# A chunked linear attention and two feed-forward layers: decay products with a floor inside the scan, and the first layer's opening blocks in turns

## The chip, the cores and the metric

One of the eight cores of a Trainium2 chip runs the whole program. The metric is the device time of one execution in microseconds (us). Engines are named as in the profile: PE is the matrix engine, PEld its weight load, DVE the vector engine, ACT the scalar engine, POOL GpSimd, and SP the engine whose queue issues all the DMAs of this kernel.

## The reference

Three stages follow one another on 3072 tokens (4 batches of 768) of width 384 (8 heads of 48).

```python
for t in range(S):                       # 768 steps, for each of 4 batches and 8 heads
    state = alpha[:, :, t, :, None] * state + einsum('bhd,bhe->bhde', k[:, :, t], v[:, :, t])
    y[:, :, t] = einsum('bhd,bhde->bhe', q[:, :, t], state)
x = y in token order, 384 wide
h = x @ w_in                             # 384 -> 2048
g = (a0 + a1 h + a2 h^2 + a3 h^3) / (1 + |b0| |h| + |b1| h^2 + 1e-6)
x = g @ w_out                            # 2048 -> 384
h = x @ w_in2;  out = (h * cos(h)) @ w_out2
```

alpha lies between 0.8 and 1. The weights arrive as 64-bit floats.

## The kernel before

**Attention.** The sequence is cut into 6 chunks of 128 steps; a chunk of one batch is one unit, so there are 24. Inside a unit, heads lie as 4 pairs (HP) on 128 partitions. decay makes the running product p of the decays along the chunk, four rows of 128 in one tensor_tensor_scan (L246): state = a * state + fresh, where fresh is 0 but for each row's first column, which holds the row's first decay (and a[..., 0] is 0, so the scan starts anew there). guess1 (L261) writes max(p, 2^-60) to the bank r and sums it; guess2 (L268, L269) turns r into exp(-ln r) on ACT and sums that; inverse0 (L276) and inverse1 (L284) refine the inverse by one step, and inverse0 sums r * p. q is multiplied by p (scale_q, L293) and k by the inverse (scale_k, L288), both on POOL, after which a unit is a masked product of scores plus a product with the state. The sums go to three rows of chk; all_ok0 and all_ok1 test them in units 16 and 18 of the layers and set a flag. Were it set, a general path (general) would run after the fast one.

attention(n, tick) writes one turn of this pipeline: for unit n the scores, for n+1 scale_q, the inverse and scale_k, for n+2 the guesses, for n+3 the decay, for n-1 and n-2 the output and the update of the state. The order on each engine is the order of the program text, written by hand; every engine works through its own queue in that order.

**Layers.** Two layers of 96 units each: 6 blocks of 512 tokens, and for each block 16 groups of 128 features. A unit is gemm1 (9 matmuls at L478: weights and x each split into a high and a low part, three products over three slices of 128) and, five units later in the first layer and four in the second, gemm2 (9 matmuls at L491 into three accumulators acc0 to acc2). Between them, rational or cosine work on the unit's 128 x 512 values on DVE, ACT and POOL, spread over the following units; L539 is the last reader of a unit's bank b0, b1 or b2, which gemm1 takes again three units on. At a block's end acc_out copies the accumulators and stores them. x of the next block is loaded by x_load and split by x_hi (ACT) and x_lo (DVE, L603). The layers' unit 0 is written right behind attention unit 20 (LEAD), so attention units 20 to 24 and layer units 0 to 4 are interleaved.

**Weights.** Each of 64 weight tiles (128 x 384, 64 bit) is fetched by w_fetch into one of four slots of a spare x tile or one of two raw tiles, turned to 32 bit in three steps (step 0: L66 and L67 on ACT; step 1: L71 and step 2: L72 on DVE), and split into high (L182, ACT) and low (L191, POOL). tick(k, ahead) takes up to k steps where it stands, as long as more than ahead tiles are under way. During the attention, step 0 writes to the one bank words_t; from unit 0 of the layers on, the steps work in SBUF alone until the second layer. w_order is the order of the tiles: for the first layer, feature i of w_in and feature i - 4 of w_out side by side. The first 16 tiles of the second layer are parked in DRAM (wd), with kq_t and v_t as staging, and loaded back by w_load from unit 80 on.

**Fetches.** In the attention units from 0 on, before: one fetch a unit (two where n is a multiple of 4). In the first 16 units of the layers: up to two fetches and two steps a unit. After that: one of each.

Of the kernel before, what the change touches and what calls it, by code (L numbers as in the profile page):

```python
# [23 lines left out]
NU = NC * B  # L24
NO = 0
# [13 lines left out]
def attn_then_two_moe(ctx, tc, kqT, aT, vP, w1i, w1o, ma, mb, w2i, w2o, out):  # L39
# [56 lines left out]
    def bank(tag, shape=(128, TB), dtype=F32):  # L96
# [8 lines left out]
    chk = const.tile([128, 3, NU + 1], F32, name="chk")  # L105
# [11 lines left out]
        [(0, s, i) for i in range(NF) for s in range(2)], key=lambda w: (w[2] + 4 * w[1], w[1])  # L117
    ) + [(1, s, i) for s in range(2) for i in range(NF)]
    spare = x_p.tile([128, 2, NK, TB], F32R, tag="x", name="spare").rearrange("p a b c -> p (a b c)").bitcast(I32)
# [8 lines left out]
    def in_spare(i):  # L128
        return i < 24 and i % 6 < 4
# [55 lines left out]
    def w_lo(engs):  # L185
        engs = list(engs)
        while to_lo:
            (m, s, i), hi = to_lo.pop(0)
            at = early(m, s, i)
            lo = ws[s][i][:, 1] if at is None else v_t[at % 3][:, :DM].bitcast(F32R)  # L190
            engs[0].tensor_tensor(  # L191
                out=lo, in0=stage.pop((m, s, i)), in1=hi.bitcast(F32), op=ALU.subtract
            )
            engs.append(engs.pop(0))
            if at is not None:
# [3 lines left out]
    def w_load(at):  # L199
        nc.sync.dma_start(out=ws[at // NF][at % NF].bitcast(F32), in_=wd[at])  # L200
# [38 lines left out]
    def decay(u):  # L239
# [4 lines left out]
        for hs in parts(u):  # L244
            nc.vector.tensor_tensor(out=fresh[:, hs, 0:1], in0=first[:, hs], in1=fresh[:, hs, 1:2], op=ALU.add)
            nc.vector.tensor_tensor_scan(  # L246
                d["p"][:, hs].rearrange("p a b -> p (a b)"), rest[:, hs].rearrange("p a b -> p (a b)"),
                fresh[:, hs].rearrange("p a b -> p (a b)"), 0.0, ALU.mult, ALU.add,
            )

    def last_decay(u):
        d = U[u]
        d["pc"] = in_p.tile([128, HP, 1], F32, tag="pc", name="pc", bufs=6)
        nc.vector.tensor_tensor(out=d["pc"], in0=d["p"][:, :, C - 1:], in1=fresh[:, :, 1:2], op=ALU.add)


    def guess1(u):
# [7 lines left out]
    def guess2(u):  # L265
        for hs in parts(u):
# [12 lines left out]

    def inverse1(u, hs):  # L280
# [3 lines left out]
        nc.vector.scalar_tensor_tensor(d["n"][:, hs], d["m"][:, hs], -2.0, d["r"][:, hs], ALU.add, ALU.mult)  # L284
# [110 lines left out]
    def attention(n, tick):  # L395
# [28 lines left out]
        if n not in (-1, 0) and on(n + 2):  # L424
            guess1(n + 2)
# [3 lines left out]
        if n in (-2, -1):  # L429
            guess1(n + 3)  # L430
# [9 lines left out]
        if n not in (-1, 0) and on(n + 2):  # L440
            guess2(n + 2)
        if n in (-2, -1):
            guess2(n + 3)
# [21 lines left out]
    def where(n):  # L465
        m, r = divmod(n, N1)
        return m, *divmod(r, NF)

    def gemm1(n):
        m, blk, f = where(n)  # L470
        h = bank(f"b{n % 3}")
# [10 lines left out]
    def gemm2(n):  # L482
        m, blk, f = where(n)
        d = T.pop(n)
        for k in range(NK):
            if f == 0:
# [3 lines left out]
            for i, (w, g) in enumerate(((0, "hi"), (0, "lo"), (1, "hi"))):  # L490
                nc.tensor.matmul(  # L491
                    acc[k], ws[1][f][:, w, ks], d[g], start=f == 0 and i == 0, stop=f == NF - 1 and i == 2
                )
            if f == NF - 1:
                outs.append((m, blk, k))
# [3 lines left out]
    def acc_out(most=NK):  # L499

        while outs and most:
            most -= 1
            m, blk, k = outs.pop(0)
# [102 lines left out]
    ok = const.tile([128, 3, NU], F32, name="ok")  # L606

    def all_ok0():
        nc.vector.tensor_tensor(out=chk[:, :, 0], in0=chk[:, :, 0], in1=chk[:, :, NU], op=ALU.add)
        nc.vector.tensor_scalar(ok[:, 0:2, :], chk[:, 0:2, :NU], RANGE, None, ALU.is_le)  # L610
        nc.vector.tensor_scalar(ok[:, 2, :], chk[:, 2, :NU], -float(HP * C), None, ALU.add)
        nc.vector.tensor_tensor(out=ok[:, 2, :], in0=ok[:, 2, :], in1=ok[:, 2, :], op=ALU.mult)
        nc.vector.tensor_scalar(ok[:, 2, :], ok[:, 2, :], 0.0625, None, ALU.is_le)

    def all_ok1():
        cnt = bank("r1", (1, 3 * NU))
# [3 lines left out]
        nc.vector.tensor_scalar(bad, tot, 128.0 * 3 * NU - 0.5, None, ALU.is_lt)  # L620


    def layers(n):
# [13 lines left out]
        split = f in (11, 12, 13) and n < 2 * N1 and nxt[0] < 2  # L637
# [3 lines left out]
        if split:  # L641
            x_hi(*nxt, f - 11)
        second(n)
        if n < 2 * N1 and nxt[0] < 2 and f == 8:
            for kk in range(NK):
                x_load(*nxt, kk)
        if split:
            x_lo(*nxt, f - 11)
# [28 lines left out]
    with tc.manual_schedule():  # L677
# [3 lines left out]
        nc.vector.memset(fresh, 0.0)  # L681
# [12 lines left out]
        for n in range(-3, NU + 1):  # L694
# [3 lines left out]
            if n >= 0:  # L698
# [5 lines left out]
                for i in range(min(n, 1) if n % 4 else 2):  # L704
# [211 lines left out]
```

## Time and profile before

| | |
|---|---|
| three timed runs | 965.59, 962.27, 965.47 us; median 965.47 |
| the profiled execution | 963.49 us, of which the span of its instructions is 961.7 |
| busy, share of the span | PE 96%, PEld 78%, DVE 70%, ACT 68%, POOL 64% |
| DMA | 84.54 MB, most of it in the first 150 us |

The shares are means over unlike stages: the attention up to about 130 us, the hand-over with the layers' first units, and the layers to the end. Each stage has a bound of its own, so stages are read one by one. In rows of groups, the time after the bar is idle time of the engine ahead of them and what ended it; in a timeline the same stands in brackets.

### The profile page before, as it was taken

How to read it: one execution, taken by the hardware profiler on the slowest of the kernel's cores; microseconds unless marked ns; L12 is line 12 of the kernel's file. 1: busy time of each engine (PE TensorE's matmuls, PEld its weight loads, DVE VectorE, ACT ScalarE, POOL GpSimd, SP SyncE). 2: the span in 40 equal slices, each digit the busy share in tenths (PEclk: the TensorE clock that was granted, in tenths of full speed). 3: DMA queues.
4: the chain of work that ended last, by engine and by line, in shares of the span. 5: the costliest groups of instructions: out<-in, count | busy, mean ns of one | idle time of the engine just before them, and what ended most of it. 6: DMA issues, size and time to landing. Idle time of an engine off the chain costs nothing.

```text
span 961.7 us, 14225 instructions
## 1 busy us (share of the span) xinstructions
PE 925.4 (96%) x4976; PEld 745.8 (78%) x4976; DVE 668.8 (70%) x1089; ACT 654.2 (68%) x1196; POOL 612.2 (64%) x559
## 2 busy tenths in 40 slices
PE   7788799999999999999999999999999999999997
PEld 6677677778888888888888888888888888888885
DVE  8989889999999998989979956434334334343331
ACT  5888888878888878888777877554444444454442
POOL 4888899978998889989878755423232332333232
PEclk7988999999999999999999999999999999999999
DMA  7999853202213114022044233010100100100001
GB/s 230 316 299 286 262 184 87 89 2 91 74 58 124 33 51 131 33 100 82 33 140 157 83 121 109 1 66 1 35 32 1 66 1 1 66 1 1 33 1 36
DMA packets 47008, 84.54 MB, mean 88 GB/s; under 512 B 5521, under 2 KB 22161, under 8 KB 46929
## 3 DMA queue, kind: packets, MB, share of 16 engines
q1 hardware_dynamic: 46928, 83.55, 27.2%
q8 instruction: 41, 0.67, 0.3%
q14 instruction: 39, 0.31, 0.1%
HBM read 63.09 MB, written 20.45 MB: 87 GB/s over the span
## 4 chain that ended last, share of the span: by engine, by line
PE 80%; DVE 10%; DMA 4%; issue 2%; POOL 2%; ACT 1%; SPq 0%; DVEq 0%; ACTq 0%; POOLq 0%
PE acc L491 39%; PE b L478 38%; DMA v<-vP 2%; DVE p L246 1%; DVE st L72 1%; DMA spare<-w1o 1%; DVE z L536 1%; DVE g L552 1%; DVE r L541 1%; DVE g L539 1%; DVE z L284 1%; POOL kq L288 1%; DMA a<-aT 1%; DVE ah L276 1%; PE sc L301 1%
## 5 line engine op out<-in xcount | busy, mean ns | idle before, releaser
L521 POOL TENSOR_TENSOR lo<-g,hi 128x512 fp32r<-128x512 f32 x192 | 257.7, 1342 | 299.4 <-ACT hi L516 292.9
L478 PE MATMUL b<-x,w 128*128 128x512 f32 x1728 | 435.3, 396 | 3.7 <-DVE g L539 3.7
L491 PE MATMUL acc<-hi,w 128*128 128x512 f32 x1152 | 392.6, 396 | 0.0
L478 PEld LDWEIGHTS b<-x,w 128*128 128x128 f32 x1728 | 323.9, 188 | 84.2 <-DVE g L539 6.2
L491 PEld LDWEIGHTS acc<-hi,w 128*128 128x128 f32 x1152 | 216.5, 188 | 52.3
L516 ACT ACTIVATE hi<-g 128x512 fp32r<-128x512 f32 x192 | 121.3, 632 | 185.4 <-PE acc L491 118.9
L491 PE MATMUL acc<-lo,w 128*128 128x512 f32 x576 | 227.8, 395 | 0.0
L568 DVE TENSOR_TENSOR g<-ah,b 128x512 f32<-128x512 f32 x96 | 65.7, 684 | 140.3 <-ACT ah L566 140.3
L547 POOL TENSOR_TENSOR z<-z,ah 128x512 f32<-128x512 f32 x96 | 124.9, 1301 | 8.0
L491 PEld LDWEIGHTS acc<-lo,w 128*128 128x128 f32 x576 | 108.3, 188 | 26.1
L78 DVE SCALAR_TENSOR_TENSOR ah<-z,b 128x512 f32<-128x512 int32 x96 | 65.7, 684 | 37.6 <-ACT z L77 37.6
L77 ACT ACTIVATE z<-b 128x512 int32<-128x512 f32 x96 | 57.0, 594 | 50.1 <-PE b L478 50.1
L548 DVE TENSOR_TENSOR g<-g,b 128x512 f32<-128x512 f32 x96 | 65.1, 678 | 24.7 <-ACT g L545 24.5
L546 POOL TENSOR_SCALAR z<-ah,cq 128x512 f32<-128x512 f32 x96 | 75.2, 783 | 1.6 <-ACT ah L544 1.6
L545 ACT ACTIVATE g<-b,cq 128x512 f32<-128x512 f32 x96 | 74.6, 777 | 0.0
L552 DVE SCALAR_TENSOR_TENSOR g<-g,cq,r 128x512 f32<-128x512 f32 x96 | 70.7, 737 | 0.1
L539 DVE SCALAR_TENSOR_TENSOR g<-g,cq,b 128x512 f32<-128x512 f32 x96 | 70.5, 735 | 0.0
L566 ACT ACTIVATE ah<-ah,half_pi 128x512 f32<-128x512 f32 x96 | 68.1, 709 | 0.0
L556 ACT ACTIVATE r<-z,lnb 128x512 f32<-128x512 f32 x96 | 66.7, 695 | 0.0
L541 DVE SCALAR_TENSOR_TENSOR r<-z,r 128x512 f32<-128x512 f32 x96 | 65.4, 681 | 0.0
L536 DVE SCALAR_TENSOR_TENSOR z<-z,r 128x512 f32<-128x512 f32 x96 | 64.8, 675 | 0.3 <-ACT kq L182 0.3
L544 ACT ACTIVATE ah<-b 128x512 f32<-128x512 f32 x96 | 56.4, 588 | 6.5 <-PE b L478 6.4
(109 smaller groups left out, 987.6 us busy)
## 6 DMA issues: line engine op xcount, KB each, us to landing
kq<-kqT SPq DMA_DIRECT2D x24, 512.0 KB, 5.2
raw<-w2i SPq DMA_DIRECT2D x16, 384.0 KB, 3.1
raw<-w2o SPq DMA_DIRECT2D x16, 384.0 KB, 3.1
w<-wd SPq DMA_DIRECT2D x16, 384.0 KB, 3.1
v<-vP SPq DMA_DIRECT2D x24, 192.0 KB, 4.5
x<-x0d SPq DMA_DIRECT2D x18, 256.0 KB, 3.7
x1d<-o SPq DMA_DIRECT2D x18, 256.0 KB, 2.2
x<-x1d SPq DMA_DIRECT2D x18, 256.0 KB, 3.5
```

The source lines that it names most:

```text
L478: nc.tensor.matmul(h, ws[0][f][:, w, ks], x[:, xx, kk, :], start=i == 0, stop=i == 8)
L491: nc.tensor.matmul(acc[k], ws[1][f][:, w, ks], d[g], start=f == 0 and i == 0, stop=f == NF - 1 and i == 2)
L516: nc.scalar.activation(out=t["hi"], in_=t["g"], func=AF.Copy)
L521: eng.tensor_tensor(out=t["lo"], in0=t["g"], in1=t["hi"].bitcast(F32), op=ALU.subtract)
L536: nc.vector.scalar_tensor_tensor(z, z, ONE_EPS, r, ALU.add, ALU.mult)
L539: nc.vector.scalar_tensor_tensor(g, g, cq[:, 3:4], two["h"], ALU.add, ALU.mult)
L541: nc.vector.scalar_tensor_tensor(r, z, -2.0 / LN_S, r, ALU.add, ALU.mult)
L545: nc.scalar.activation(out=g, in_=h, func=AF.Identity, scale=cq[:, 5:6], bias=cq[:, 4:5])
L546: nc.gpsimd.tensor_scalar(zz, ah, cq[:, 1:2], cq[:, 0:1], ALU.mult, ALU.add)
L547: nc.gpsimd.tensor_tensor(out=zz, in0=zz, in1=ah, op=ALU.mult)
L552: nc.vector.scalar_tensor_tensor(g, g, cq[:, 2:3], r, ALU.add, ALU.mult)
L566: nc.scalar.activation(out=two["r"], in_=two["r"], func=AF.Sin, bias=half_pi)
```

## The change

The scan gets a maximum for its second operation, and fresh holds the floor 2^-60 instead of 0: state = max(a * state, fresh). p then never falls below the floor, guess1 is left out, and ACT's Ln reads p itself. The sum that guess1 made is dropped, and the sum of the inverse is taken in inverse1 instead of Ln/Exp, so chk has two rows instead of three.

The first layer's blocks 0 and 1 take turns: units 0 to 9 are block 0's features 0 to 9, units 10 to 19 block 1's, then six features of block 0 and six of block 1. At each of these ends acc_out parks partial sums in kq_t (part), and the last six features' sums are added to them by DVE. The order of the tiles follows. In units 2 to 31 there is one fetch and (from unit 3) one step a unit, with one tile kept ahead. The attention makes a second fetch in units 0, 7 and 14 only, and none after unit 20. Block 1's x is loaded in unit 3 and split in units 5 to 7, block 2's in units 26 and 28 to 30. The second layer's tiles therefore start in unit 32 instead of 16.

```diff
+H1 = 10
-    chk = const.tile([128, 3, NU + 1], F32, name="chk")
+    chk = const.tile([128, 2, NU + 1], F32, name="chk")
-        [(0, s, i) for i in range(NF) for s in range(2)], key=lambda w: (w[2] + 4 * w[1], w[1])
+        [(0, s, i) for i in range(NF) for s in range(2)],
+        key=lambda w: (w[2] + 5 * w[1] + (H1 if w[2] >= H1 else 0), w[1])
...
-        return i < 24 and i % 6 < 4
+        return i < 22 and i % 6 < 4
...
-            nc.vector.tensor_tensor(out=fresh[:, hs, 0:1], in0=first[:, hs], in1=fresh[:, hs, 1:2], op=ALU.add)
+            nc.vector.tensor_tensor(out=fresh[:, hs, 0:1], in0=first[:, hs], in1=fresh[:, hs, 1:2], op=ALU.max)
             nc.vector.tensor_tensor_scan(
                 d["p"][:, hs].rearrange("p a b -> p (a b)"), rest[:, hs].rearrange("p a b -> p (a b)"),
-                fresh[:, hs].rearrange("p a b -> p (a b)"), 0.0, ALU.mult, ALU.add,
+                fresh[:, hs].rearrange("p a b -> p (a b)"), 0.0, ALU.mult, ALU.max,
             )
...
-            nc.vector.tensor_scalar(
-                d["r"][:, hs], d["p"][:, hs], P_MIN, None, ALU.max, ALU.add, accum_out=sums(1, u, hs)
-            )
...
-            r = U[u]["r"][:, hs]
-            nc.scalar.activation(out=r, in_=r, func=AF.Ln)
-            nc.scalar.activation(out=r, in_=r, func=AF.Exp, scale=-1.0, accum_out=sums(0, u, hs))
+            nc.scalar.activation(out=d["r"][:, hs], in_=d["p"][:, hs], func=AF.Ln)
+            nc.scalar.activation(out=d["r"][:, hs], in_=d["r"][:, hs], func=AF.Exp, scale=-1.0)
...
-            d["m"][:, hs], d["r"][:, hs], 1.0, d["p"][:, hs], ALU.mult, ALU.mult, accum_out=sums(2, u, hs)
+            d["m"][:, hs], d["p"][:, hs], RANGE, d["r"][:, hs], ALU.min, ALU.mult, accum_out=sums(1, u, hs)
...
-        nc.vector.scalar_tensor_tensor(d["n"][:, hs], d["m"][:, hs], -2.0, d["r"][:, hs], ALU.add, ALU.mult)
+        nc.vector.scalar_tensor_tensor(
+            d["n"][:, hs], d["m"][:, hs], -2.0, d["r"][:, hs], ALU.add, ALU.mult, accum_out=sums(0, u, hs)
+        )
...
+        if n < 2 * H1:
+            return 0, *divmod(n, H1)
+        if n < 2 * NF:
+            blk, f = divmod(n - 2 * H1, NF - H1)
+            return 0, blk, H1 + f
...
+    def part(blk, k):
+        return kq_t[2 * blk + k // 2][:, k % 2].rearrange("p a b -> p (a b)")
...
+        first = f == 0 or in_parts(m, blk) and f == H1
+        last = f == NF - 1 or in_parts(m, blk) and f == H1 - 1
...
+            if f < NF - 1:
+                nc.scalar.activation(out=part(blk, k), in_=acc[k], func=AF.Copy)
+                continue
             o = in_p.tile([128, TB], F32, tag="p", name="o")
-            if m == 1 and k == 1:
+            if in_parts(m, blk):
+                nc.vector.tensor_tensor(out=o, in0=part(blk, k), in1=acc[k], op=ALU.add)
+            elif m == 1 and k == 1:
                 nc.vector.tensor_copy(o, acc[k])
...
-        split = f in (11, 12, 13) and n < 2 * N1 and nxt[0] < 2
+        at, load = f - 11, f == 8
+        if n < NF:
+            nxt, at, load = (0, 1), n - 5, n == 3
+        elif n < 2 * NF:
+            at, load = f - 12, f == 10
+        split = 0 <= at < NK and n < 2 * N1 and nxt[0] < 2
...
-        if n < NF:
-            for _ in range(2):
+        if n < 2 * NF:
+            if n > 1:
                 w_fetch(2 * NF)
-            tick(0 if n < 4 else 2)
+                tick(1 if n > 2 else 0, 1)
...
-        nc.vector.memset(fresh, 0.0)
+        nc.vector.memset(fresh, P_MIN)
...
-                for i in range(min(n, 1) if n % 4 else 2):
+                for i in range((min(n, 1) if n % 7 else 2) if n <= LEAD else 0):
                     w_fetch(2 * NF)
```

## Rows read from the trace of the kernel before

**Rows 1.** Stages: us, then each engine's busy us (instructions), PE's granted clock, DMA share, GB/s.
```profile
8.00:16.00 8.00, 5.23 (x29) 4.50 (x29) 7.62 (x22) 3.55 (x9) 2.16 (x3) 0.50 0.59 172
...
28.00:104.00 76.00, 64.04 (x854) 53.05 (x852) 66.97 (x160) 63.49 (x142) 65.33 (x70) 0.89 0.93 292
...
151.00:217.50 66.50, 62.80 (x267) 48.51 (x264) 64.39 (x95) 53.29 (x96) 60.34 (x53) 1.00 0.18 51
...
800.00:900.00 100.00, 100.00 (x430) 80.60 (x429) 37.94 (x53) 47.82 (x80) 30.94 (x24) 1.00 0.07 24
```

**Rows 2.** Timeline of PE (start us, us, instruction, idle ahead): two layer units' first matmuls.
```profile
154.26 1.90 PE L478 MATMUL b<-x,w 128*128 128x512 f32 x7 [0.79 <-DVE g L539]
...
217.56 2.26 PE L478 MATMUL b<-x,w 128*128 128x512 f32 x9
...
221.76 0.63 PE L478 MATMUL b<-x,w 128*128 128x512 f32 x2
```

**Rows 3.** Timeline of DVE in a plain interval of the attention.
```profile
72.61 0.08 DVE L276 DVE_READ_ACCUMULATOR ah<-r,p 128x1 f32 x1
...
73.45 0.69 DVE L261 TENSOR_SCALAR_CACHE_REDUCE r<-p 128x512 f32<-128x512 f32 x1
...
74.06 0.21 DVE L245 TENSOR_TENSOR r<-a,r 128x4 f32<-128x4 f32 x1
74.38 1.22 DVE L246 TENSOR_TENSOR_SCAN p<-a,r 128x512 f32<-128x512 f32 x1
```

**Rows 4.** Timeline of DVE in one of the four long intervals.
```profile
79.39 1.22 DVE L246 TENSOR_TENSOR_SCAN p<-a,r 128x512 f32<-128x512 f32 x1
...
84.57 0.69 DVE L276 SCALAR_TENSOR_TENSOR ah<-r,p 128x512 f32<-128x512 f32 x1 [1.05 <-ACT r L269]
...
86.64 0.55 DVE L72 SCALAR_TENSOR_TENSOR st<-spare,b 128x384 int32<-128x384 int32 x1
...
87.37 1.22 DVE L246 TENSOR_TENSOR_SCAN p<-a,r 128x512 f32<-128x512 f32 x1
```

**Rows 5.** Timeline of DVE: three of the eighteen scans between 28 and 127 us.
```profile
28.07 1.22 DVE L246 TENSOR_TENSOR_SCAN p<-a,r 128x512 f32<-128x512 f32 x1
...
104.35 1.22 DVE L246 TENSOR_TENSOR_SCAN p<-a,r 128x512 f32<-128x512 f32 x1
...
126.72 1.22 DVE L246 TENSOR_TENSOR_SCAN p<-a,r 128x512 f32<-128x512 f32 x1
```

**Rows 6.** Timeline of ACT in the same long interval.
```profile
81.82 0.51 ACT L67 ACTIVATE b<-spare 128x384 int32<-128x384 uint8 x1 [1.58 <-DVE st L72]
...
83.22 0.60 ACT L268 ACTIVATE r<-r 128x512 f32<-128x512 f32 x1
```

**Rows 7.** Timeline of POOL: the first mask of two attention units.
```profile
71.62 0.63 POOL L313 TENSOR_SCALAR_AFFINE_SELECT hi<-hi 128x512 f32<-128x512 f32 x1
...
76.24 0.64 POOL L313 TENSOR_SCALAR_AFFINE_SELECT hi<-hi 128x512 f32<-128x512 f32 x1
```

**Rows 8.** DMA from 28 to 104 us, and from 60 to 80 us.
```profile
DMA packets 11420, 22.19 MB, mean 292 GB/s; under 512 B 1864, under 2 KB 5064, under 8 KB 11408
...
DMA packets 4088, 6.46 MB, mean 323 GB/s; under 512 B 449, under 2 KB 2401, under 8 KB 4086
```

**Rows 9.** One group of DVE from 151 to 217 us: busy us, mean ns.
```profile
L72 DVE SCALAR_TENSOR_TENSOR st<-raw,st 128x384 int32<-128x384 int32 x6 | 8.7, 1453 | 0.1
```

**Rows 10.** Timelines of POOL and PE in the second layer's unit 101.
```profile
568.10 1.03 POOL L191 TENSOR_TENSOR w<-st,w 128x384 fp32r<-128x384 f32 x1
...
570.36 0.39 PE L491 MATMUL acc<-hi,w 128*128 128x512 f32 x1
```

**Rows 11.** Two more stages, columns as in rows 1.
```profile
43.00:57.00 14.00, 12.07 (x142) 10.03 (x144) 13.02 (x32) 11.03 (x26) 13.11 (x14) 0.76 0.91 288
...
84.00:98.00 14.00, 11.53 (x132) 9.59 (x132) 13.01 (x32) 11.16 (x26) 13.05 (x15) 0.76 0.86 266
```

**Rows 12.** The chain that ended last (start us, us, what), one piece.
```profile
92.67 1.90 PE b L364 x16
```

More of the change, by code (lines that the diff above doesn't have):

```diff
@@ L116, in attn_then_two_moe @@
     w_order = sorted(
-        [(0, s, i) for i in range(NF) for s in range(2)], key=lambda w: (w[2] + 4 * w[1], w[1])
+        [(0, s, i) for i in range(NF) for s in range(2)],
+        key=lambda w: (w[2] + 5 * w[1] + (H1 if w[2] >= H1 else 0), w[1])
     ) + [(1, s, i) for s in range(2) for i in range(NF)]
+    ready = set()
     spare = x_p.tile([128, 2, NK, TB], F32R, tag="x", name="spare").rearrange("p a b c -> p (a b c)").bitcast(I32)
@@ L194, in w_lo @@
             engs.append(engs.pop(0))
+            ready.add((m, s, i))
             if at is not None:
@@ L199, in w_load @@
     def w_load(at):
+        assert (1, at // NF, at % NF) in ready
         nc.sync.dma_start(out=ws[at // NF][at % NF].bitcast(F32), in_=wd[at])
@@ L253, in last_decay, with guess @@
         d["pc"] = in_p.tile([128, HP, 1], F32, tag="pc", name="pc", bufs=6)
-        nc.vector.tensor_tensor(out=d["pc"], in0=d["p"][:, :, C - 1:], in1=fresh[:, :, 1:2], op=ALU.add)
-    def guess1(u):
+        nc.vector.tensor_tensor(out=d["pc"], in0=d["p"][:, :, C - 1:], in1=fresh[:, :, 1:2], op=ALU.max)
+    def guess(u):
         d = U[u]
@@ L423, in attention @@
                 tick(0 if on(n + 2) else 1)
-        if n not in (-1, 0) and on(n + 2):
-            guess1(n + 2)
         tick(1)
@@ L428, in attention @@
             decay(n + 3)
-        if n in (-2, -1):
-            guess1(n + 3)
         tick(1)
@@ L440, in attention @@
         if n not in (-1, 0) and on(n + 2):
-            guess2(n + 2)
+            guess(n + 2)
         if n in (-2, -1):
-            guess2(n + 3)
+            guess(n + 3)
         if on(n - 1):
@@ L466, in where, with in_parts @@
         m, r = divmod(n, N1)
+        if n < 2 * H1:
[3 more added lines that the diff above has]
+            return 0, blk, H1 + f
         return m, *divmod(r, NF)
+    def in_parts(m, blk):
+        return m == 0 and blk < 2
+    def part(blk, k):
+        return kq_t[2 * blk + k // 2][:, k % 2].rearrange("p a b -> p (a b)")
     def gemm1(n):
         m, blk, f = where(n)
+        assert m or (0, 0, f) in ready
         h = bank(f"b{n % 3}")
@@ L484, in gemm2 @@
         d = T.pop(n)
+        assert m or (0, 1, f) in ready
+        first = f == 0 or in_parts(m, blk) and f == H1
+        last = f == NF - 1 or in_parts(m, blk) and f == H1 - 1
         for k in range(NK):
-            if f == 0:
+            if first:
                 acc_out()
@@ L491, in gemm2 @@
                 nc.tensor.matmul(
-                    acc[k], ws[1][f][:, w, ks], d[g], start=f == 0 and i == 0, stop=f == NF - 1 and i == 2
+                    acc[k], ws[1][f][:, w, ks], d[g], start=first and i == 0, stop=last and i == 2
                 )
-            if f == NF - 1:
-                outs.append((m, blk, k))
+            if last:
+                outs.append((m, blk, f, k))
     outs = []
@@ L603, in x_lo @@
         nc.vector.tensor_tensor(out=lo, in0=lo.bitcast(F32), in1=hi.bitcast(F32), op=ALU.subtract)
-    ok = const.tile([128, 3, NU], F32, name="ok")
+    ok = const.tile([128, 2, NU], F32, name="ok")
     def all_ok0():
         nc.vector.tensor_tensor(out=chk[:, :, 0], in0=chk[:, :, 0], in1=chk[:, :, NU], op=ALU.add)
[L610 to L613, printed above, removed]
+        nc.vector.tensor_scalar(ok[:, 0, :], chk[:, 0, :NU], -RANGE, None, ALU.is_ge)
+        nc.vector.tensor_scalar(ok[:, 1, :], chk[:, 1, :NU], -float(HP * C), None, ALU.add)
+        nc.vector.tensor_tensor(out=ok[:, 1, :], in0=ok[:, 1, :], in1=ok[:, 1, :], op=ALU.mult)
+        nc.vector.tensor_scalar(ok[:, 1, :], ok[:, 1, :], 0.0625, None, ALU.is_le)
     def all_ok1():
-        cnt = bank("r1", (1, 3 * NU))
+        cnt = bank("r1", (1, 2 * NU))
         nc.tensor.matmul(cnt, ones, ok.rearrange("p a b -> p (a b)"), start=True, stop=True)
@@ L641, in layers @@
         if split:
-            x_hi(*nxt, f - 11)
+            x_hi(*nxt, at)
         second(n)
-        if n < 2 * N1 and nxt[0] < 2 and f == 8:
+        if n < 2 * N1 and nxt[0] < 2 and load:
             for kk in range(NK):
@@ L647, in layers @@
         if split:
-            x_lo(*nxt, f - 11)
+            x_lo(*nxt, at)
         i = n - (N1 - NF)
-        if n < NF:
-            for _ in range(2):
+        if n < 2 * NF:
+            if n > 1:
                 w_fetch(2 * NF)
-            tick(0 if n < 4 else 2)
+                tick(1 if n > 2 else 0, 1)
         elif n < N1 - NF:
```

6 lines of the change are left out of this document (2 added, 4 removed).

## The prediction, made before the changed kernel was run

> **What bounds the kernel now.** I read busy time by stage first [rows 1], then the matrix engine's timeline. From 217.56 on, one unit of the layers (nine matmuls at L478, nine at L491) starts every 4.20 us [rows 2] and PE is busy 100 of 100 us: nothing in the diff changes those matmuls, so that stage can only begin earlier. Time is to be had in two places. Between 151 and 217.5 PE is busy 62.80 of 66.5 us, so 3.7 us are idle, and the idle time ends on DVE's L539, as the 0.79 us ahead of 154.26 [rows 1, 2]: there DVE is busy 64.39 of 66.5 us. And before unit 0 of the layers the attention runs, where DVE is busiest (66.97 of 76 us) with DMA close behind (0.93 of its engines) [rows 1].
>
> DVE's timeline of the attention shows how. The scan recurs every 5.01 us (74.38 to 79.39) with no idle time in between [rows 3, 4]; eight of the 17 intervals between the scans at 28.07 and 126.72 [rows 5] are like this. Four others are long (7.25, 9.03, 7.98, 7.98 us). The one from 79.39 to 87.37 is typical: two tiles had been fetched for that unit, so a second tile's first step was put behind the first tile's last. Its ACT half, L67, waits 1.58 us for DVE's L72 [rows 6], because both tiles use the one bank words_t; ACT is then late with Ln and Exp, DVE waits 1.05 us for them at 84.57, and a left-over step at 86.64 delays the scan [rows 4]. The remaining five intervals take 4.36 to 6.23 us.
>
> **The change, part by part.**
>
> *guess1 goes.* Its slot on DVE runs from 73.45 to the start of L245 at 74.06, 0.61 us [rows 3]; L245 then starts free of its accumulator read, about 0.05 us more. inverse1 gains an accumulator read, 0.08 us by L276's [rows 3]. Net -0.58 us: a plain interval of DVE goes from 5.01 to 4.43 us. On ACT one accumulator read goes, and Ln reads p in SBUF where it read r in PSUM: 0.60 us now, at 83.22 [rows 6]. I take that unchanged, and for bounds +-0.2 us, a third of the row either way; ACT is not last in a plain interval, so nothing hangs on it. Ln no longer waits for DVE; the scan two units ahead is long done.
>
> What is late next? POOL: its five operations of a unit fill 71.62 to 76.24 back to back, 4.62 us [rows 7]. And DMA: from 28 to 104 it moved 22.19 MB at 292 GB/s, while the 20 us from 60 to 80 moved 323 GB/s [rows 8]; 22.19 / 323 is 68.7 us, so of these 76 us at most 7.3 can go. I take 4.65 us for a plain interval.
>
> *The scan's second operation, max for add.* No row shows it. Lower end: a plain two-input operation, 0.69 us (L276 at 84.57) [rows 4]. Upper end: the scan's 1.22 us [rows 3] plus two more passes of 0.69, 2.60 us. I take 1.22, the row of the same instruction with the same operands. [...]
>
> *Tile fetches.* By the code, attention units 3 to 19 before convert 20 tiles, after 19; double fetches come at units 0, 4, 8, 12, 16 before and at 0, 7, 14 after. The counts are nearly the same, so DMA, DVE, ACT and POOL save one tile; what goes is two of four long intervals, with their waits of 1.58 and 1.05 us. A long one should shrink to 6.6: 4.65, two extra DVE steps of 0.47 each start to start, and a wait of about 1.0.
>
> *The sum for 28.07 to 126.72,* 98.65 us now: 15 intervals at 4.65 are 69.8, two at 6.6 are 13.2, and I leave 3 for waits such as those behind the 5.73 and 6.23 us intervals: 86, a gain of 12.7. DMA's limit cuts this: 7.3 at most before 104, and after it four intervals (from 104.35, 22.4 us now [rows 5]) that become 18.6, 3.8: 11.1 together. As that rate is not held for 76 us in a row, I take 9, bounds 4 (the eight plain intervals at 0.37 and one long one less) and 11.1.
>
> [...] Of 6 x 0.58 = 3.5 us I take 2, bounds 0 and 3.5.
>
> *The layers' first 25 units.* Of the first layer's 32 tiles the last is ready in unit 25 instead of unit 12, one step a unit. In units 4 to 12 DVE has six steps where it had ten; the three x_lo come in units 5 to 7 instead of 11 to 13. At about 1.2 us each (under the 1.45 of L72 in this stage, as L71 is the shorter) [rows 9] and with 0 to 1 x_lo more inside, that is 3.5 us less by unit 13; by unit 19 the steps before and after differ by one, and PE is 100% busy from there as it was. So of PE's 3.7 us idle I take 3 as gone, bounds 0 and 3.7. What is added lies beside other work: six copies of partial sums go to ACT where six copies of results were, and six adds to DVE, 0.7 us each, in units 31 to 37, where no weight step runs after unit 25 until 33 (DVE frees 0.4 us or more a unit). If that cover were gone they would cost at most 4 us once. all_ok0 and all_ok1 lose a third of their columns: nothing. x_load of block 1 now stands in unit 3 on SP, behind only the store of a finished unit, and takes the spare tile, last read in attention unit 20; block 2's, in unit 26, waits for the last matmul of unit 25 and holds up only later weight fetches.
>
> *The second layer's weights* start 16 units later. Its w_out tiles 1 to 15 come ready one unit ahead of their matmuls instead of four. Now such a tile is done on POOL at 568.10 + 1.03 = 569.13, and the matmuls that would need it then start at 570.36: 1.2 us to spare [rows 10]. I take 0; as much later once, it costs 0 to 2 us, since one wait of PE gives all later tiles the same room.
>
> **Sum:** 963.49 for the profiled execution, - 2 - 9 - 3 = 949.5. The median of the runs shown is 965.47 and they spread from 962.27 to 965.59, so I put half of the 2 us on top: **950.5**.
>
> **Rivals.**
> *DMA and the order on SP hold (0.17).* For: share 0.93 already, and SP's one queue holds every load behind a wait for a buffer. Against: plain intervals have no DVE idle time. Then the attention gains 4, the layers 1 to 2, the start 0: 958.
> *The low clock goes too (0.15).* [...]
> *No change (0.08).* The attention's gain is taken back at the hand-over, where POOL's masks, products and weight remainders of units 20 to 23 run back to back and one remainder moves ahead of them: 960.7 to 965.
> *Slower (0.03).* max costs two more passes in the scan: 2.60 us. An interval becomes 5.01 - 0.58 + 1.38 = 5.81, 23 of them 18 us more, against 4 from the fewer long intervals and 3 in the layers: 975. It decides from about 0.6 us above 1.22.
> *The change doesn't do what it says:* were the new test of the sums to fail, the general path would run as well, with a time of another order; alphas between 0.8 and 1 keep the products far above the floor, so I give it no weight.
>
> **How the numbers follow.** Forecast 0.57, the rivals as marked. Own range of the forecast: bounds 963.5 - 18.3 and - 4, so 946 to 960.5. Taking in the clock rival and the DMA rival, 8 in 10 lie in 943.5 to 959.5. Faster by over 0.5%, about what a measurement here can tell from no change (below 960.6): 0.57 + 0.17 + 0.15 = 0.89; within 0.5%: 0.08; slower: 0.03.
>
> **What would show it.** Right: scans 4.4 to 4.8 us apart, with POOL without idle time or DMA at its limit beside them; two long intervals instead of four, at units 7 and 14; the scan still 1.22 us; unit 0 of the layers some 11 us earlier; PE without idle from about unit 5; 4.20 us a unit to the end. Wrong: plain intervals still near 5 us; a scan longer than 1.22; PE waiting for L539 in units 5 to 19 as now, or for w_out's remainders near unit 100.

## The result and the profile after

The changed kernel took **949.62 us** (median of four runs, 945.51 to 954.28) against 963.87 us for the kernel before on the same chip (961.43 to 965.59): a ratio of 0.9855, 95% interval 0.9828 to 0.9881. The forecast was 950.5 us. The profiled execution took 952.98 us with a span of 951.3. Lines have moved: L71, L72, L245, L246, L276, L284, L478 and L539 of before are L72, L73, L250, L251, L275, L283, L488 and L557 now.

The windows of the changed kernel answer to [rows 1] (us, then each engine's busy us and instructions, PE's granted clock, DMA share, GB/s):

```profile
8.00:16.00 8.00, 6.56 (x61) 5.75 (x61) 7.62 (x20) 3.67 (x7) 4.15 (x5) 0.79 0.75 228
28.00:104.00 76.00, 67.90 (x892) 56.13 (x894) 59.67 (x153) 63.59 (x131) 67.91 (x73) 0.87 0.93 296
60.00:100.00 40.00, 34.92 (x538) 29.06 (x538) 36.65 (x93) 38.11 (x79) 39.08 (x43) 1.00 0.98 315
147.50:207.50 60.00, 59.46 (x256) 47.24 (x255) 58.02 (x88) 49.48 (x89) 53.57 (x48) 1.00 0.10 30
800.00:900.00 100.00, 100.00 (x430) 80.57 (x429) 36.95 (x53) 47.67 (x79) 30.49 (x24) 1.00 0.07 24
```

DVE is busy 59.67 us of the same 76, where it had 66.97: it is no longer the busiest engine of the attention. From 60 to 100 us POOL is busy 39.08 of 40 us, ACT 38.11, and DMA has a share of 0.98. In the layers' first units PE is busy 59.46 of 60 us; the stage of the second layer is the same. (Of the 84.54 MB that the kernel before moves, 38.62 MB fall in its first 150 us: less than half, not most.)

A plain interval on DVE, against [rows 3], from one scan to the next:

```profile
71.14 0.69 DVE L275 SCALAR_TENSOR_TENSOR ah<-p,r 128x512 f32<-128x512 f32 x1
71.87 0.69 DVE L283 SCALAR_TENSOR_TENSOR z<-ah,r 128x512 f32<-128x512 f32 x1
72.48 0.08 DVE L283 DVE_READ_ACCUMULATOR z<-ah,r 128x1 f32 x1
72.48 0.16 DVE L250 TENSOR_TENSOR r<-a,r 128x4 f32<-128x4 f32 x1
72.75 1.22 DVE L251 TENSOR_TENSOR_SCAN p<-a,r 128x512 f32<-128x512 f32 x1
...
75.90 0.69 DVE L275 SCALAR_TENSOR_TENSOR ah<-p,r 128x512 f32<-128x512 f32 x1 [0.43 <-ACT r L267]
...
77.51 1.22 DVE L251 TENSOR_TENSOR_SCAN p<-a,r 128x512 f32<-128x512 f32 x1
```

guess1 is gone, and the scan with its maximum takes the same 1.22 us. The interval is 4.76 us, and now DVE waits in it: 0.43 us for ACT's Exp. Between the scans at 59.30 and 117.41 the intervals are 4.25 to 5.44 us, but for one of 7.24; without that one their mean is 4.63. Two of them, 5.44 and 5.21, hold an x_lo; the nine plain ones are 4.25 to 4.83, with a mean of 4.47.

The long interval at unit 14, against [rows 4, 6], DVE and then ACT:

```profile
87.20 1.22 DVE L251 TENSOR_TENSOR_SCAN p<-a,r 128x512 f32<-128x512 f32 x1
...
90.26 0.56 DVE L72 SCALAR_TENSOR_TENSOR b<-st,b 128x384 int32<-128x384 int32 x1 [0.26 <-ACT b L68]
90.73 0.69 DVE L621 TENSOR_TENSOR x<-x 128x512 fp32r<-128x512 f32 x1
92.36 0.69 DVE L275 SCALAR_TENSOR_TENSOR ah<-p,r 128x512 f32<-128x512 f32 x1 [0.95 <-ACT r L267]
...
93.71 0.55 DVE L73 SCALAR_TENSOR_TENSOR st<-spare,b 128x384 int32<-128x384 int32 x1
...
94.44 1.22 DVE L251 TENSOR_TENSOR_SCAN p<-a,r 128x512 f32<-128x512 f32 x1
```

```profile
89.70 0.53 ACT L68 ACTIVATE b<-spare 128x384 int32<-128x384 uint8 x1 [0.87 <-DVE st L73]
```

It is built like the one before: two tiles through the one bank words_t, ACT late by 0.87 us, DVE then waiting 0.95 us for Ln and Exp, a left-over step ahead of the scan. L621 is x_lo (L603 of before).

The profiled execution also has an early stretch that before had in a smaller form [rows 11]. Its chain of waits (start us, us, what) and one window of it (columns as above):

```profile
19.37 7.48 DMA kq<-kqT
...
33.66 1.05 PE b L322 x4
34.71 1.03 PE u L334 x16
35.73 2.01 PE sc L302 x16
37.74 1.90 PE b L365 x16
39.64 1.90 PE b L375 x16
41.55 1.05 PE b L322 x4
```

```profile
32.00:48.00 16.00, 16.00 (x140) 13.39 (x138) 9.57 (x25) 10.43 (x22) 13.98 (x16) 0.50 0.90 282
```

One load of kq took 7.48 us; after the lull that it left, PE ran from 30.4 to 50.9 us at a granted 0.50 and was the bound there with 7.89 us a unit (33.66 to 41.55), busy all of the 16 us of the window.

At the other end of the stage, against [rows 2], the unit that started at 217.56 now starts at 207.48, and the next 4.20 us on:

```profile
207.48 2.26 PE L488 MATMUL b<-x,w 128*128 128x512 f32 x9
...
211.68 1.56 PE L488 MATMUL b<-x,w 128*128 128x512 f32 x6
```

For the experiments I cut every profiled execution into five stretches: from the start to the eighth scan (28.07 in [rows 5]), on to the last scan (126.72), on to unit 5 of the layers (154.26 in [rows 2]), on to unit 19 (217.56), and to the end. Times in us:

| kernel | to 8th scan | attention | hand-over, to unit 5 | units 5 to 19 | rest |
|---|---|---|---|---|---|
| before | 28.07 | 98.65 | 27.54 | 63.30 | 744.1 |
| changed | 24.13 | 93.28 | 30.09 | 59.98 | 743.8 |
| after_again | 24.43 | 86.75 | 33.03 | 60.00 | 743.3 |
| scan_only | 24.39 | 93.92 | 28.87 | 63.26 | 744.3 |
| turns_only | 28.13 | 96.40 | 28.09 | 60.51 | 743.4 |
| dma_less | 24.00 | 88.09 | 28.29 | 60.42 | 744.2 |
| words_late | 24.70 | 92.41 | 28.16 | 60.44 | 743.6 |
| words_ok | 24.57 | 88.02 | 28.13 | 59.26 | 744.4 |
| words_ok_even | 24.88 | 84.87 | 31.78 | 58.80 | 744.7 |

Each row is one execution, and the attention of one and the same kernel differs by 6.5 us between two of them; verdicts rest on the timed runs.

### The profile page after: what moved, and what is told of

It is laid out like the page before. It is cut to its first block, busy times and chain, and to the rows that moved or that the text cites. A ratio compares the mean times of both kernels' runs of the same rounds, so it can differ in the third digit from the quotient of the medians.

```text
span 951.3 us, 14178 instructions
## 1 busy us (share of the span) xinstructions
PE 925.7 (97%) x4976; PEld 747.1 (79%) x4976; DVE 649.5 (68%) x1070; ACT 651.9 (69%) x1171; POOL 611.9 (64%) x559
## 2 busy tenths in 40 slices
DMA packets 47007, 84.54 MB, mean 89 GB/s; under 512 B 5520, under 2 KB 22160, under 8 KB 46928
## 4 chain that ended last, share of the span: by engine, by line
PE 83%; DVE 7%; ACT 4%; DMA 2%; issue 2%; POOL 0%; SPq 0%; DVEq 0%; ACTq 0%; POOLq 0%
PE acc L504 40%; PE b L488 40%; DVE p L251 1%; DMA a<-aT 1%; PE sc L302 1%; DVE st L72 1%; DMA kq<-kqT 1%; PE b L375 1%; PE u L334 1%; DVE ah L275 1%; DVE g L570 1%; DVE st L73 1%; PE b L365 1%; ACT g L563 0%; DVE g L557 0%
## 5 line engine op out<-in xcount | busy, mean ns | idle before, releaser
L539 POOL TENSOR_TENSOR lo<-g,hi 128x512 fp32r<-128x512 f32 x192 | 257.1, 1339 | 295.0 <-ACT hi L534 288.6
L488 PE MATMUL b<-x,w 128*128 128x512 f32 x1728 | 436.2, 397 | 0.5 <-DVE g L557 0.5
L488 PEld LDWEIGHTS b<-x,w 128*128 128x128 f32 x1728 | 325.2, 188 | 79.9 <-DVE g L557 1.2
L565 POOL TENSOR_TENSOR z<-z,ah 128x512 f32<-128x512 f32 x96 | 127.4, 1328 | 8.0
L557 DVE SCALAR_TENSOR_TENSOR g<-g,cq,b 128x512 f32<-128x512 f32 x96 | 70.7, 737 | 0.0
```

The source lines that it names most:

```text
L488: nc.tensor.matmul(h, ws[0][f][:, w, ks], x[:, xx, kk, :], start=i == 0, stop=i == 8)
L539: eng.tensor_tensor(out=t["lo"], in0=t["g"], in1=t["hi"].bitcast(F32), op=ALU.subtract)
L557: nc.vector.scalar_tensor_tensor(g, g, cq[:, 3:4], two["h"], ALU.add, ALU.mult)
L565: nc.gpsimd.tensor_tensor(out=zz, in0=zz, in1=ah, op=ALU.mult)
```

## The experiments

All were timed in five rounds beside the kernel before. The medians of the kernel before were 963.18 us for the first four, 962.58 for the next four and 962.91 for the last four.

### The two halves by themselves, and the whole once more

scan_only is the kernel before with the scan's part of the change (max in the scan, no guess1, two sums instead of three); turns_only is the kernel before with the rest (turns of blocks 0 and 1, order and times of the fetches, x loaded and split earlier); after_again is the changed kernel.

```
scan_only:
-            nc.vector.tensor_scalar(
-                d["r"][:, hs], d["p"][:, hs], P_MIN, None, ALU.max, ALU.add, accum_out=sums(1, u, hs)
-            )
...
-                fresh[:, hs].rearrange("p a b -> p (a b)"), 0.0, ALU.mult, ALU.add,
+                fresh[:, hs].rearrange("p a b -> p (a b)"), 0.0, ALU.mult, ALU.max,
...
turns_only:
+        if n < 2 * H1:
+            return 0, *divmod(n, H1)
...
-            tick(0 if n < 4 else 2)
...
+                tick(1 if n > 2 else 0, 1)
...
-                for i in range(min(n, 1) if n % 4 else 2):
+                for i in range((min(n, 1) if n % 7 else 2) if n <= LEAD else 0):
```

> The scan's half of the change alone (floor inside the scan, no guess1, two sums), with the tiles, fetches and blocks of before. By my sum: a plain interval of the attention falls from 5.01 to about 4.65 us, the four long intervals stay, the layers' idle 3.7 us stay: 6 to 9 us faster than before. Rival, the order of loads: the interval is set by DMA and by what waits on SP, so that DVE's relief shows as idle time: 0 to 4 us faster. Second rival, the clock: with the same program the time spreads by 7 us or more with the granted clock (0.98 against 0.99), and the half's own share is small beside it.

> The other half alone: blocks 0 and 1 in turns, one weight tile a unit, double fetches at units 0, 7, 14, with guess1 and the scan of before. By my sum: two of four long intervals go (4 to 5 us) and 3 us of PE's idle time at units 5 to 19: 7 us faster than before, plain intervals still 5.0 us. Rival: the fetches' order gives nothing, since each long interval that goes comes back as a wait for a load: 3 us faster. The two halves should add up to the whole change's 14 us within 3 us if they are independent.

> The changed kernel as it is, for more runs on one chip with the others. If the clock sets the spread: runs fall into two groups, near 946 with a granted clock of about 0.993 and near 953 with 0.982 to 0.986, and time and clock go together run by run. If not: a spread without that order.

Measured: scan_only 951.31 us (ratio 0.9878, 0.9853 to 0.9903), turns_only 957.18 (0.9933, 0.9912 to 0.9955), after_again 948.47 (0.9848, 0.9825 to 0.9871). That is -11.9, -6.0 and -14.7 us. scan_only gave more than the 6 to 9 us expected of it, turns_only about the 7; the halves add up to 17.9, 3.2 more than the whole gives, a little over the 3 that were allowed for independent halves; with intervals of some 2 us either way on each, this doesn't show that they depend on each other. The two groups of runs expected of after_again, split by the clock, didn't show (see "The low clock").

The table says where each half works. The 3.7 us before the eighth scan are the scan's alone. The 3 us in units 5 to 19 are the turns' alone: in scan_only PE still waits for DVE there as before, in turns_only that wait is nearly gone (waits of PE in these units; us in total, times, longest; scan_only, then turns_only):

```profile
PE b L470 <- DVE g L531: 3.5, 5, 1.4
```

```profile
PE b L496 <- DVE g L565: 0.5, 1, 0.5
```

What is left of the two gains, some 8 us of scan_only's and 3 of turns_only's, belongs to the attention and the hand-over. In the table both halves shorten the attention, by 4.7 and 2.3 us, but that is one execution each. So both reasons of the forecast hold, each for its half.

### What is late next in the attention

Four kernels change the load of one resource at a time in the changed kernel: pool_more does each unit's second mask twice, dma_more fetches v a second time into a tile that nobody reads, dve_more does inverse0 twice, and dma_less fetches only half of the bytes of the 16 weight tiles that go to the spare tile.

```
pool_more:
-        for s in U[u]["s"]:
+        for s in U[u]["s"] + U[u]["s"][1:]:
dma_more:
...
+            nc.sync.dma_start(out=v_x[u % 3], in_=src)
dve_more (once more):
+        nc.vector.scalar_tensor_tensor(
+            d["m"][:, hs], d["p"][:, hs], RANGE, d["r"][:, hs], ALU.min, ALU.mult, accum_out=sums(1, u, hs)
+        )
dma_less:
+        part_of = slice(0, DM if in_spare(i) else 2 * DM)
...
```

> The changed kernel with the second of POOL's two masks done twice in each attention unit, about 0.6 us more on POOL, 24 times, 14.4 us in all. If POOL is what is late next after guess1 went (4.62 us a unit, as I put it): 10 to 14 us slower than the changed kernel's 948.5. If DMA is: 0 to 4 us. If waits between the engines' queues set the pace rather than one engine: 5 to 9 us here and as much for each of the other two.

> The changed kernel with each unit's v fetched a second time, into a tile that nothing reads: 192 KB, 0.61 us of DMA at 323 GB/s, 24 times, 14.6 us in all. If DMA's limit holds from 28 to 104 (the cut that I made from 12.7 to 9): 8 to 14 us slower than 948.5. If POOL or DVE set the pace and the loads only run ahead: 0 to 4 us.

> The changed kernel with inverse0's operation done twice, 0.6 to 0.7 us more on DVE in each unit, 24 times, 14 to 17 us in all, about what guess1 cost. If DVE stays the bound: 14 to 17 us slower than 948.5, more than the scan's half of the change gave (12). If DVE has 0.2 us to spare in a unit against POOL: 8 to 11 us. If DMA holds: 0 to 5 us.

> The changed kernel with only half of the bytes of each weight tile that goes to the spare tile (16 of the first 24 tiles; the other half stays zero, so part of the weights is left out of what is computed): 3.1 MB less of DMA before the layers, every instruction of the other engines as before, but for four fills on POOL at the start. Theory 'DMA sets the pace of the attention, POOL is next': at 324 GB/s 3.1 MB is 9.7 us; plain intervals fall to POOL's 4.65 us and no lower, and the time falls by 3 to 7 us against the changed kernel's 948.47. Rival 'the intervals are set by the engines' order, DMA is only busy beside them': under 1.5 us.

Measured: pool_more 956.38 us (0.9930, 0.9916 to 0.9943), dma_more 959.82 (0.9964, 0.9951 to 0.9977), dve_more 954.72 (0.9919, 0.9901 to 0.9937). Against after_again they cost 7.9, 11.3 and 6.2 us of the 14.5 or so that each adds. All three resources are near the bound, DMA nearest. No one theory holds for all of them: dma_more's cost lies in the range of a limit by DMA (8 to 14), pool_more's in that of waits between the queues (5 to 9, and as much for each of the others), and dve_more's in none of its three. But dma_less took 948.63 us (0.9848, 0.9823 to 0.9873), the time of after_again: the theory 'DMA sets the pace' expected 3 to 7 us less, and the rival under 1.5. The windows (columns as above) show how small the relief was; first after_again, then dma_less:

```profile
24.00:110.00 86.00, 76.71 (x1121) 63.46 (x1121) 78.31 (x191) 78.63 (x162) 80.97 (x87) 0.96 0.98 318
60.00:100.00 40.00, 35.74 (x539) 29.39 (x535) 37.58 (x92) 37.79 (x78) 37.77 (x40) 1.00 1.00 324
```

```profile
24.00:110.00 86.00, 76.31 (x1102) 62.66 (x1098) 76.39 (x187) 77.38 (x159) 80.93 (x86) 0.96 0.94 297
60.00:100.00 40.00, 35.97 (x520) 29.87 (x522) 37.91 (x91) 36.61 (x76) 38.62 (x41) 0.96 0.97 303
```

In after_again DMA is at a share of 1.00 and 324 GB/s for 40 us in a row, with DVE, ACT and POOL at 37.6 to 37.8 of 40 us each. With fewer bytes the rate falls to 303 GB/s and the share only to 0.97; more of the packets are small (from 24 to 110 us 7807 under 2 KB, where after_again has 5970). POOL is at 38.62 of 40 us, and nothing is faster. The relief in DMA's own time was small (0.04 of 86 us, 3.4 us), so this run doesn't show that DMA costs nothing; that POOL and the order of the engines stand right behind it is argued from the busy times, not shown. Adding to any of the three costs less than what is added, so none of them alone is the bound all the time; the one relief that was tried, of DMA, gained nothing, and POOL and ACT were not relieved in the attention.

### The low clock

after_fill puts four small matmuls ahead of the scores of units 1 to 9, to fill PE's lulls there.

```
+        if 1 <= u <= 9:
+            for i in range(4):
+                nc.tensor.matmul(d["sc"][0][:, i, :], ident, ident, start=True, stop=True)
```

> The changed kernel with four more 128x128 matmuls of the identity ahead of the scores of attention units 1 to 9, into the bank that the scores overwrite. They use PE where it waits for POOL. If lulls of PE at units 2 to 4 bring the low clock that then holds for some 20 us: the clock stays up, granted 0.99 or more in all runs, and all runs are at 944 to 948. [...]

Measured: 950.40 us (0.9873, 0.9849 to 0.9896), 1.9 us over after_again. The granted clock stayed up through the attention, and at 0.991 to 0.995 over whole runs, as the theory of the lulls said; but the runs took 948.43 to 952.20 us, not 944 to 948:

```profile
24.00:60.00 36.00, 34.31 (x474) 28.86 (x473) 28.76 (x72) 30.53 (x64) 31.63 (x35) 1.00 0.96 307
60.00:100.00 40.00, 34.86 (x532) 28.87 (x532) 35.74 (x88) 36.42 (x76) 38.06 (x41) 1.00 1.03 329
```

No time was gained, so a few us at a granted 0.50, as after_again has them (6.9 us, 0.96 on average), are hardly what holds the attention; what the 36 fillers themselves cost isn't told apart from what they gave. That a longer stretch costs is another matter. Of the table's six kernels with both halves of the change, the two whose profile has a long one in the attention, 20.5 us in the changed kernel's and 13.6 in words_late's, have the longest attentions, 93.28 and 92.41 us; the other four, with 6.9 us at most at a time, have 84.87 to 88.09. The four runs of the changed kernel had a mean granted clock of 0.993 and 0.993 with 945.51 and 946.25 us, 0.982 and 0.986 with 952.98 and 954.28. In after_again that order is gone: the run with the highest clock, 0.993, was the slowest of the five (949.91), and three at 0.991 took 946.23 to 948.47. Over 69 runs in thirteen series, each run against its own series' mean, 0.001 less of the clock goes with 0.50 us more (correlation -0.62). The kernel before had 0.984 (median of its 33 runs beside the experiments), after_again 0.991; by that slope some 3.5 of the 14.7 us go along with the clock. Whether the clock makes them or a lull makes both isn't told apart.

### The hand-over

The table has a loss that the forecast doesn't: from the last scan to unit 5 the changed kernel takes 2.6 and 5.5 us more than before. rest_dve moves the weights' low parts of these units from POOL to DVE. words_late keeps the steps of the weights on the bank words_t for two units longer.

```
rest_dve:
...
-            w_lo([nc.gpsimd])
+            w_lo([nc.vector if n >= LEAD - 1 else nc.gpsimd])
words_late:
-        if slot[0] < LEAD:
+        if slot[0] < LEAD + 2:
```

> The changed kernel with the weights' low parts on DVE instead of POOL from attention unit 19 to layer unit 4, where POOL is busy 19.2 of 20 us and DVE 13.3. If POOL holds up the hand-over (units 0 to 4 of the layers take 2 us more than before, and unit 0 follows its scan 1 to 4 us later): 2 to 5 us faster than 948.5. If PE's own work sets it (5.43 us a unit): within 1 us, as POOL's idle time grows.

> The changed kernel, in which the weight steps keep the bank words_t for two units longer (attention units 20 and 21), so that DVE's L72 there reads one operand from the bank and not two from SBUF; nothing else. Observed in the changed kernel's run (948.47 us): at 112.31 us this L72 took 4.77 us, while POOL worked back to back from 110.83 to 116.67, and PE then stood idle 4.80 us ahead of the layers' unit 0. Theory 'the two SBUF operands made L72 wait for POOL': it takes about 0.55 us again, PE's 4.8 us idle shrink under 1 us, unit 0 of the layers starts about 4 us earlier, and the time falls by 3 to 4.5 us, to 944 to 945.5. Rival 'L72 waited for something else, such as its tile or ACT': the row stays near 4.8 us and the time at 948 to 949. Rival 'the hand-over units are bound by PE's own work': the row shrinks but the units 0 to 4 take as much longer, and the time falls by less than 1.5 us.

Measured: rest_dve 949.86 us (0.9850, 0.9830 to 0.9871), no gain where 2 to 5 us were expected if POOL held the hand-over, which takes 29.91 us here. words_late 946.44 us (0.9822, 0.9807 to 0.9837), 2.0 us under after_again, where 3 to 4.5 were expected; the two intervals overlap, so the gain isn't clear of noise. Its mechanism is in the timelines. after_again, DVE and then POOL and PE:

```profile
111.18 1.22 DVE L251 TENSOR_TENSOR_SCAN p<-a,r 128x512 f32<-128x512 f32 x1
112.31 4.77 DVE L72 SCALAR_TENSOR_TENSOR st<-st,spare 128x384 int32<-128x384 int32 x1
117.01 0.35 DVE L346 TENSOR_TENSOR u<-s,u 128x192 f32<-128x192 f32 x1
```

```profile
112.02 1.28 POOL L294 TENSOR_TENSOR kq<-kq,p 128x512 f32<-128x512 f32 x1
113.26 1.27 POOL L289 TENSOR_TENSOR kq<-kq,z 128x512 f32<-128x512 f32 x1
114.48 0.64 POOL L314 TENSOR_SCALAR_AFFINE_SELECT hi<-hi 128x512 f32<-128x512 f32 x1
115.06 0.64 POOL L314 TENSOR_SCALAR_AFFINE_SELECT lo<-lo 128x512 f32<-128x512 f32 x1
115.67 1.00 POOL L194 TENSOR_TENSOR w<-st,w 128x384 fp32r<-128x384 f32 x1
118.45 1.03 POOL L194 TENSOR_TENSOR w<-st,w 128x384 fp32r<-128x384 f32 x1 [1.78 <-ACT w L185]
```

```profile
118.23 1.10 PE L334 MATMUL u<-v,g 128*64 128x48 f32 x16 [4.80 <-DVE pc L259]
119.26 3.44 PE L488 MATMUL b<-x,w 128*128 128x512 f32 x9
```

From attention unit 20 on the steps have no bank, and L72 reads two operands from SBUF. It took 4.77 us and ended at 117.08, 0.41 us after POOL's row of five operations without a gap; what DVE had queued behind it, the update of the state, came as much later, and PE stood idle 4.80 us ahead of the layers' unit 0. The 4.77 us reach over five of POOL's operations, the first of them under way when L72 began (112.02 to 116.67). In the changed kernel's first profile the same L72 took 1.63 us, ending at 120.18, 0.42 after a POOL operation behind which POOL paused. In words_late, where one operand comes from the bank:

```profile
118.25 0.54 DVE L72 SCALAR_TENSOR_TENSOR b<-st,b 128x384 int32<-128x384 int32 x1
```

```profile
119.92 0.67 PE L334 MATMUL u<-v,g 128*64 128x48 f32 x16 [0.55 <-DVE pc L259]
120.52 2.37 PE L488 MATMUL b<-x,w 128*128 128x512 f32 x9
```

0.54 us, PE idle 0.55 us, and a hand-over of 28.16 us, 28.13 in words_ok, near the 27.54 of before. By itself this row leaves a rival open: POOL ended an operation at 118.54 and then paused for 2.16 us, so its dense row of after_again did not recur. Other rows settle it. In after_again itself, just ahead of the long L72, a step with one operand in the bank ran wholly beside an operation of POOL, in its usual time:

```profile
108.64 1.28 POOL L289 TENSOR_TENSOR kq<-kq,z 128x512 f32<-128x512 f32 x1
108.65 0.56 DVE L73 SCALAR_TENSOR_TENSOR st<-spare,b 128x384 int32<-128x384 int32 x1
```

Over the first 260 us of all 14 profiles, the steps with one operand in a bank took 0.53 to 0.60 us (580 rows, most of them beside a busy POOL). Those with both in SBUF took 0.53 to 0.55 us where POOL was idle (14 rows); where it was busy they took up to 1.70 us, and once 4.77. All 189 of over 0.8 us ended 0.4 us after the end of a POOL operation, 182 of them after the one that was running when they began, though in most cases POOL's next operation followed at once. So that such a step waits for POOL is shown; a wait over five operations occurred once, and why that one lasted over five is open.

Behind the idle time came a second loss. In after_again PE's granted clock was 0.50 from 118.2 to 121.7 us, and unit 0's nine matmuls took 3.44 us; in words_late it stayed at 1.00 and they took 2.37. The changed kernel's first profile has the same: PE 1.85 us idle, then 0.50 from 122.6 to 126.0 us and 3.80 us for the nine. dma_less, with an L72 of 1.08 us and no such stretch, has a hand-over of 28.29 us.

The median gained less than the 4.9 us between the hand-overs of these two executions, which fits an L72 as long as 4.77 us being the exception: in the profiles of the other kernels that have it without the bank it took 0.53 to 1.64 us.

### Two attempts at a better version

words_ok is words_late with the test of the sums ten units later; words_ok_even also spreads the two second fetches over units 21 and 22.

```
words_ok:
-        if n == NF:
+        if n == NF + 10:
...
words_ok_even:
...
-                for i in range((min(n, 1) if n % 7 else 2) if n <= LEAD else 0):
+                for i in range((min(n, 1) if n else 2) if n <= LEAD + 2 else 0):
```

> The kernel of the run before in this list, with the two steps that test the sums (all_ok0, all_ok1) moved from units 16 and 18 of the layers to units 26 and 28. In the changed kernel the periods of units 16 to 18 are 4.93, 4.30 and 4.57 us against 4.20 around them, 1.2 us together. If these steps of DVE and PE cause them, the time falls by about 1.2 us below the run before; if units 26 to 28 lose the same (block 2's x is split there), by 0.

> The kernel of the run before in this list, with the second fetches in attention units 7 and 14 moved: one fetch a unit in units 1 to 22 instead (two in unit 0 stays). The long intervals at units 5 to 7 and 14 (7.07, 7.60 and 7.23 us in the changed kernel's run) should then be plain ones. If they are long because of the second tile's steps, the attention gains 2 x (7.4 - 4.8) = 5 us at most; if DMA's rate sets the pace (its share is 1.00 from 60 to 100 us), only the two moved tiles' time counts, 0.39 MB each at 324 GB/s, 1.2 us each, so 2.4 us; and the two steps that now stand in the hand-over may give some of it back. I expect 1 to 3 us less than the run before.

Measured: words_ok **945.34 us** (0.9812, 0.9799 to 0.9826), the fastest median here: 3.1 us under after_again, whose interval only just overlaps. Of the step from words_late, 1.1 us, the trace bears out little. The periods of units 16 to 18 fall from 4.90, 4.30 and 4.57 to 4.20 us, 1.2 us, but those of units 28, 31 and 32 are now 4.57, 4.77 and 4.30, 1.0 us more: the loss is moved. words_ok_even took 946.89 us (0.9824, 0.9803 to 0.9844) where 1 to 3 us less were expected. The long intervals are gone and its attention is the shortest of all, 84.87 us; but the moved steps stand in the hand-over, where one unit now takes 10.7 us and the stretch 31.78 instead of 28.13. What the attention gave was taken back.

## Why the prediction was right, point by point

The time came within 1 us of the forecast, but two terms of its sum (-2, -9, -3) measured otherwise and one loss had no term, so that the total came out so near is in part luck. The two places where time was to be had, and the two halves that take it there, were right.

- **The start** (-2, bounds 0 and 3.5) was under-sized: 3.6 to 3.9 us, above its upper bound, and scan_only shows that all of it is the scan's half. That only 2 of its 3.5 us would come was my estimate, and no run shows a reason for it: from 8 to 16 us PE's granted clock was 0.50 before and 0.79 in the changed kernel, DVE was busy 7.62 of the 8 us in both, and all of the 3.5 us came. And guess1's net 0.58 us was too little: where DVE works back to back in both kernels, scans were 3.70 us apart (19.61 and 23.31) and are 2.93 apart (16.69 and 19.63), 0.77 us less. In part that is the accumulator read of inverse1, for which I took 0.08 us off: it starts together with L250, at 72.48 in the plain interval above, and doesn't delay it.
- **The attention** (-9, bounds 4 and 11.1) measured -5.4 in one profile and -11.9, above its upper bound, in another. The interval I took, 4.65 us, is met by the mean of 4.63, but that mean holds the two intervals with an x_lo, which I had counted as waits; the plain ones are 4.47 on average, between POOL's 4.62 and DVE's own 4.25, which is 0.76 under the 5.01 of before and not 0.58. The cut from 12.7 to 9 failed as reasoned: I took it that 323 GB/s [rows 8] would not be held, and after_again held 318 GB/s for 86 us and had its attention in 86.75 us, where the uncut sum said 86. The first profile lost its time early: from the eighth scan to the one at 59.30 (24.43 to 52.11 in after_again) it took 7.5 us more, and there lie the 20 us at a granted 0.50 after one late load, with the chain running through PE. I had the clock as a rival with a gain of its own (0.15), and no run shows how much that would be: by the slope above some 3.5 of after_again's 14.7 us go along with it, and in the first profile a long stretch at 0.50 went with a loss.
- **The long intervals** stayed at units 7 and 14, as said, and took 7.2 to 7.6 us where I had 6.6 (9.75 at unit 7 in the first profile, at the end of its stretch at a granted 0.50). The wait in them was under-sized: in the one shown DVE stands some 1.8 us behind ACT, 0.26 and 0.95 us of it idle and the rest filled by x_lo, where I had about 1.0. A third one, of 7.06 us at 33.20 in after_again, was not forecast.
- **The layers' first units** (-3) were right: from 63.30 to 59.98 us, all of it in the turns' half, PE's wait for DVE from 3.7 us to 0.5. But PE is not quite without idle time from unit 5, as I said it would be: the test of the sums takes 1.1 us in units 16 to 18 before and 1.2 us in the changed kernel, no change, as forecast.
- **The hand-over** had no term, and cost 2.6 to 5.5 us. The rival 'no change' named the place and POOL's row of operations, but thought of POOL being late; it was DVE that was held by POOL (L72 at 4.77 and 1.63 us, to 0.41 and 0.42 us after a POOL operation), then PE idle and after that at a granted 0.50, and rest_dve, which takes the remainders off POOL, gained nothing. So unit 0 of the layers, forecast some 11 us earlier, came 8.2 us earlier in the first profile and 11.1 in after_again. The row that should have warned me was in the same trace: before's L72 (L73 now) with its operands in SBUF at a mean of 1453 ns [rows 9] against 0.55 us in the attention [rows 4]. I read it as a price, not as a wait for POOL.
- **What is late next**, POOL and DMA, was right as far as both are full; that DMA alone sets a limit fits dma_more's 11.3 us and is left open by dma_less, in which the share stayed at 0.97.
- **max in the scan** and **the second layer's weights** were right at nothing: 1.22 us, and 744.1 against 743.8 us from unit 19 to the end.

So the two terms under-sized, the start and (in one of two profiles) the attention, and the missed hand-over nearly cancel: by the five stretches -3.9 -5.4 +2.6 -3.3 -0.3 = -10.4 us between the two profiled executions, -14.7 between the medians with after_again.

Open: which of lull, late load and clock comes first in the executions with a long stretch at a granted 0.50; and what holds the attention when DMA has more room than dma_less gave it.

## What to carry to other kernels

Once one engine's load is taken off and three others stand at 94 to 98% beside it, busy shares don't tell which of them sets the pace: here 14.5 us more on any of three cost 6 to 11 us, and fewer bytes gained nothing. The interval forecast from the engine next in line (POOL's 4.62 us) came near: 4.63 on average without the long one, 4.47 for the plain ones. Moving steps to a place where they look free needs a look at who runs there: here a DVE operation of 0.53 to 0.55 us with two SBUF operands took up to 1.70 us beside a busy POOL, to 0.4 us after the end of a POOL operation wherever it was over 0.8, and once 4.77; with one operand in a bank it took 0.53 to 0.60. Cut a term only for a limit that the trace shows reached; "not held for so long" was a guess and cost the forecast its reason.

## What the runs showed of the hardware that I had not expected

- A DVE operation of 0.54 us took 4.77 us beside five POOL operations without a gap, and ended 0.41 us after the last of them; in another run 1.63 us, ending 0.42 us after the POOL operation behind which POOL paused. Of 189 such operations of over 0.8 us all ended 0.4 us after the end of a POOL operation; with one operand in a bank 580 took 0.53 to 0.60 us.
- A scan that multiplies and takes the maximum costs what one that multiplies and adds costs, 1.22 us for 128x512.
- PE stayed at a granted 0.50 for 20.5 us, from 30.4 to 50.9, while its row shows it busy 16.00 of the 16 us from 32 to 48.
- The loads of this kernel kept 324 GB/s for 40 us at a share of 1.00; halving the bytes of 16 of them lowered the rate to 303 GB/s and the share only to 0.97.
